# Group normalisation on one core: stores of two groups a partition from paired half buffers

## The chip, the cores and the metric

The kernel runs on one core of one Trainium2 chip. Its time is the device time of one execution in microseconds (us), and the figure given for a kernel is the median of its runs. The kernel before the change takes 633.47 us (three runs, 633.45 to 633.54). Everything else below is read from one further execution that the hardware profiler recorded; its span, from its first instruction to its last, is 632.5 us.

## What is computed

```python
def reference(x, g, b):                      # x: 128 x 1024 x 32 x 16, bf16
    G = 32
    xr = x.reshape(B, G, C // G, H, W)
    mu = xr.mean(axis=(2, 3, 4), keepdims=True)
    var = ((xr - mu) ** 2).mean(axis=(2, 3, 4), keepdims=True)
    xn = (xr - mu) / jnp.sqrt(var + 1e-5)
    xn = xn.reshape(B, C, H, W)
    return xn * g[None, :, None, None] + b[None, :, None, None]
```

Each of the 128 samples has 32 groups of 32 channels, a channel is 512 numbers, so a group is 16,384 numbers or 32 KB, and each group is normalised by its own mean and variance. 134 MB are read and 134 MB are written.

## The kernel before

One group sits on one partition. A tile is 128 groups, which is four samples, so a tile is 128 partitions by 32 KB (4 MB) and is one unbroken stretch of memory; there are 32 tiles, numbered 0 to 31. The tiles live in a pool of six buffers (XBUFS, UPFRONT), and a tile is scaled in place in its buffer.

For tile i the main loop (the last lines of the function) does this. L(i) loads the tile, in one transfer of 32 KB a partition (line 101), or in four transfers of 8 KB a partition for the first and the last tile. M(i) multiplies the tile by an identity on TensorE (PE in the profile) in 32 matmuls into one accumulator (line 166), and R0(i) sums that on VectorE (DVE, line 189): the negative mean. Q(i) squares the tile on ScalarE (ACT, line 244) in two halves. V(i) makes a scale and a shift for each channel: a square root on ACT (line 308), a reciprocal on DVE (line 312), three small operations on GpSimd (POOL, lines 337 to 353). A(i) scales 16 of the 32 channels on DVE and 13 on POOL (line 368). The last 3 are scaled on ACT in finish(i) (line 363), which then stores the tile, S(i), in one transfer of 32 KB a partition (line 381). The last two tiles are scaled and stored in quarters of 8 KB a partition within A(i).

The order of the work is written out by hand, and a helper chains the instructions of each engine in that order. In turn i of the loop come Q(i), M(i+1), R0(i+1), V(i), A(i). Two consequences matter later. finish(i) is called inside Q(i+1), between its two halves. And R0(i+1) stands before V(i) and A(i) on DVE, so the scaling of tile i waits until tile i+1 has landed and has been summed.

All large transfers are issued from one queue, that of the sync engine (SP), and each is spread over the core's 16 DMA engines, 8 partitions to each engine. Transfers start in the order of their issue. A load into a used buffer waits, on SP, until the store out of that buffer has landed on all 16 engines, and everything behind it on SP waits with it. Before the change SP's order from then on is two stores, two loads: S(24) S(25) L(30) L(31) S(26) S(27) and so on. The variable RUN is that two.

Of the kernel before, what the change touches and what calls it, by code (L numbers as in the profile page):

```python
# [9 lines left out]
ALU = mybir.AluOpType  # L10
F32 = mybir.dt.float32
BF16 = mybir.dt.bfloat16
# [2 lines left out]
NUM_GROUPS = 32  # L15
EPS = 1e-5

XBUFS = 6
UPFRONT = 6
RUN = 2  # L20
MM_FREE = 512
QUARTERS = 4
STORE_IN_PARTS = 2
# [6 lines left out]
def kernel(  # L30
# [13 lines left out]
    nc = tc.nc  # L44
    P = nc.NUM_PARTITIONS
    B0, C, H, W = x.shape
    G = NUM_GROUPS
    HW = H * W
    assert P % G == 0 and C % G == 0
    NS = P // G  # L50
    assert B0 % NS == 0
    NT = B0 // NS
    KC = C // G
    F = KC * HW
    inv_n = 1.0 / float(F)
# [2 lines left out]
    NQ = QUARTERS  # L58
    QF = F // NQ
# [1 line left out]
    MQ = NMM // NQ  # L61
    assert NQ == 4 and F % (NQ * MMN) == 0 and KC % NQ == 0

    x_v = x.rearrange("(t n) (g k) h w -> t (n g) (k h w)", n=NS, g=G)
    o_v = out.rearrange("(t n) (g k) h w -> t (n g) (k h w)", n=NS, g=G)
    g_v = g.rearrange("(g k) -> g k", g=G)
    b_v = b.rearrange("(g k) -> g k", g=G)

    consts = ctx.enter_context(tc.tile_pool(name="consts", bufs=1))
    xpool = ctx.enter_context(tc.tile_pool(name="xpool", bufs=XBUFS))  # L70
    jpool = ctx.enter_context(tc.tile_pool(name="jpool", bufs=1))
    spool = ctx.enter_context(tc.tile_pool(name="spool", bufs=4))
    pspool = ctx.enter_context(
# [2 lines left out]
    gpool = ctx.enter_context(  # L76
        tc.tile_pool(name="gpool", bufs=1, space=bass.MemoryType.PSUM)
    )
# [6 lines left out]
    def chain(key, inst):  # L85
        prev = last.get(key)
        if prev is not None:
            tc.add_manual_dep(inst.ins, prev.ins.name, nosync, reason="pipeline order")
        last[key] = inst
        return inst  # L90

    state = {}

    def L(i):
        xt = xpool.tile([P, F], BF16, name="xt")
        parts = NQ if i == 0 or i >= NT - 1 else 1
        w = F // parts
        for c in range(parts):
            chain(
                "sp",  # L100
                nc.sync.dma_start(  # L101
                    out=xt[:, c * w : (c + 1) * w], in_=x_v[i][:, c * w : (c + 1) * w]
                ),
            )
        state[i] = {"xt": xt}

    for i in range(min(UPFRONT, NT)):
        L(i)

    gb_b = consts.tile([G, 2, KC], BF16)  # L110
    chain("act", nc.scalar.dma_start(out=gb_b[:, 0, :], in_=g_v))
    chain("act", nc.scalar.dma_start(out=gb_b[:, 1, :], in_=b_v))
    eps_t = consts.tile([P, 1], F32)
# [4 lines left out]
    ones_b = consts.tile([P, P], BF16)  # L118
# [3 lines left out]
        out=eye[:],  # L122
        in_=ones_b[:],
        pattern=[[-1, P]],
# [2 lines left out]
        base=0,  # L127
        channel_multiplier=1,
    )
    rep = consts.tile([G, P], BF16)  # L130
    nc.gpsimd.affine_select(
        out=rep[:].rearrange("q (n a) -> q n a", n=NS),
        in_=ones_b[0:G, :].rearrange("q (n a) -> q n a", n=NS),
        pattern=[[0, NS], [-1, G]],
        compare_op=ALU.is_equal,
        fill=0.0,
        base=0,
        channel_multiplier=1,
    )
    gb = consts.tile([P, 2, KC], F32)  # L140
    gam = gb[:, 0, :]
    bet = gb[:, 1, :]

    def GB():
        gb_p = gpool.tile([P, 2, KC], F32, name="gb_p")
        chain(
            "pe",
            nc.tensor.matmul(  # L148
                out=gb_p[:].rearrange("p a k -> p (a k)"),
                lhsT=rep[:],  # L150
                rhs=gb_b[:].rearrange("q a k -> q (a k)"),
                start=True,
                stop=True,
            ),
        )
        chain("dve", nc.vector.tensor_copy(out=gb[:], in_=gb_p[:]))  # L156

    def shifted(i):
        return i == 0 or i == NT - 1

# [124 lines left out]
    def V(i):  # L285
        st = state[i]
        if shifted(i):
            var = spool.tile([P, 1], F32, name="var")
            jv = spool.tile([P, NQ], F32, name="jv")
            chain(  # L290
                "dve",
                nc.vector.tensor_scalar(  # L292
                    out=jv[:],
                    in0=st["sq"][:],
                    scalar1=inv_n,
                    scalar2=st["seed"][:],
                    op0=ALU.mult,
                    op1=ALU.add,
                    accum_out=var[:],
                ),  # L300
            )
            last_sum, scale, bias = var, float(NQ * NQ), eps_t
        else:
            last_sum, scale, bias = st["s1"], inv_n, st["v0"]
        rstd = spool.tile([P, 1], F32, name="rstd")
        chain(
            "act",
            nc.scalar.activation(  # L308
                out=rstd[:], in_=last_sum[:], func=ACT.Sqrt, bias=bias[:], scale=scale
            ),  # L310
        )
        chain("dve", nc.vector.reciprocal(out=rstd[:], in_=rstd[:]))  # L312
        scl = spool.tile([P, KC], F32, name="scl")
        bia = spool.tile([P, KC], F32, name="bia")
        if i == NT - 1:
            chain(
                "dve",
                nc.vector.tensor_scalar(
                    out=scl[:], in0=gam, scalar1=rstd[:], scalar2=None, op0=ALU.mult
                ),  # L320
            )
            chain(
                "dve",
                nc.vector.scalar_tensor_tensor(  # L324
                    out=bia[:],
                    in0=scl[:],
                    scalar=st["negmean"][:],
                    in1=bet,
                    op0=ALU.mult,
                    op1=ALU.add,  # L330
                ),
            )
        else:
            shift = spool.tile([P, KC], F32, name="shift")
            chain(
                "pool",
                nc.gpsimd.tensor_scalar(  # L337
                    out=scl[:], in0=gam, scalar1=rstd[:], scalar2=None, op0=ALU.mult
                ),
            )  # L340
            chain(
                "pool",
                nc.gpsimd.tensor_scalar(  # L343
                    out=shift[:],
                    in0=scl[:],
                    scalar1=st["negmean"][:],
                    scalar2=None,
                    op0=ALU.mult,
                ),
            )  # L350
            chain(
                "pool",
                nc.gpsimd.tensor_tensor(out=bia[:], in0=shift[:], in1=bet, op=ALU.add),  # L353
            )
        st["scl"], st["bia"] = scl, bia

    def scale_on(key, i, k):
        st = state[i]
        span = st["xt"][:, k * HW : (k + 1) * HW]
        scl = st["scl"][:, k : k + 1]  # L360
        bia = st["bia"][:, k : k + 1]
        if key == "act":
            inst = nc.scalar.activation(  # L363
                out=span, in_=span, func=ACT.Identity, bias=bia, scale=scl
            )
        else:
            eng = nc.vector if key == "dve" else nc.gpsimd
            inst = eng.tensor_scalar(  # L368
                out=span,
                in0=span,  # L370
                scalar1=scl,
                scalar2=bia,
                op0=ALU.mult,
                op1=ALU.add,
            )
        chain(key, inst)

    def S(i, lo, hi):
        chain(
            "sp",  # L380
            nc.sync.dma_start(
                out=o_v[i][:, lo * QF : hi * QF],
                in_=state[i]["xt"][:, lo * QF : hi * QF],
            ),
        )

    def in_parts(i):
        return i >= NT - STORE_IN_PARTS

    def A(i):  # L390

        if not in_parts(i):
            for n in range(POOL_SHARE):
                scale_on("pool", i, KC - LAST_SHARE - POOL_SHARE + n)
            for k in range(KC - LAST_SHARE - POOL_SHARE):
                scale_on("dve", i, k)
            if i + 1 < NT:
                R1(i + 1)
            return
        for c in range(NQ):  # L400
            for k in range(c * KQ, (c + 1) * KQ):
                on_act = i == NT - 1 and k >= (c + 1) * KQ - ACT_SHARE
                scale_on("act" if on_act else "dve", i, k)
            S(i, c, c + 1)
            if c == NQ // 2 - 1 and i + 1 < NT:
                R1(i + 1)

    def finish(i):
        if i < 0 or in_parts(i):
            return  # L410
        for k in range(KC - LAST_SHARE, KC):
            scale_on("act", i, k)
        S(i, 0, NQ)
        state.pop(i)
        if i % RUN == RUN - 1:
            first = i + 1 + UPFRONT - RUN
            for j in range(first, min(first + RUN, NT)):
                L(j)

    M(0)  # L420
    R0(0)
    GB()
    R1(0)
    for i in range(NT):
# [36 lines left out]
```

## Time and profile before

| | |
|---|---|
| median of the runs | 633.47 us |
| the profiled execution's span | 632.5 us |
| HBM read and written | 134.22 MB each, 424 GB/s over the span |
| busy ACT | 537.9 us (85% of the span) |
| busy DVE | 379.0 us (60%) |
| busy POOL | 345.3 us (55%) |
| busy PE | 260.9 us (41%) |
| loads of 4096 KB, issue to landing, median | 19.4 us (30 of them) |
| stores of 4096 KB, issue to landing, median | 29.3 us (30 of them) |
| loads and stores of 1024 KB | 8 each, 11.5 and 17.9 us |

Busy times are sums over the span for each engine. The time from issue to landing holds the time that a transfer spends in the queue behind earlier ones. The page also has the chain that ended last, which goes back from the last instruction to whatever released it; in this execution 62% of that chain is DMA, 15% ACT and 9% PE.

### The profile page before, as it was taken

The page shows a single profiled execution, that of the slowest core. Times are in us where ns is not written, and L with a number is a line of the kernel's source. Part 1 is how long each engine was busy: PE and PEld are TensorE (multiplying, and loading weights), DVE is VectorE, ACT ScalarE, POOL GpSimd, SP SyncE. Part 2 cuts the span into 40 slices and gives each one's busy share as a digit, 9 for nine tenths or more (in the row PEclk, how much of TensorE's full clock was granted, in tenths as well). Part 3 has the DMA queues.
Part 4 walks back from the last instruction along what each step waited for, and adds up shares of the span by engine and source line. Part 5 has one row for each costly group of instructions (what it writes and reads, how often), then busy time and mean ns, then how long its engine had stood idle before and what let it go on. Part 6 is the DMA issues. An engine that isn't in the chain of part 4 may idle for free.

```text
span 632.5 us, 3907 instructions
## 1 busy us (share of the span) xinstructions
PE 260.9 (41%) x1025; PEld 106.4 (17%) x1025; DVE 379.0 (60%) x645; ACT 537.9 (85%) x268; POOL 345.3 (55%) x523
## 2 busy tenths in 40 slices
PE   5577609064180632806327063270723607146000
PEld 2223203021030210302113021030301203012000
DVE  1077766666676477563665636666466663657660
ACT  4599999999999699696996969969798796987960
POOL 0077776666666377563665636666365663657100
PEclk9789759668595675957759577595875958758555
DMA  9999999999999999999999999999999999999996
GB/s 371 437 428 406 436 433 431 433 429 433 429 424 433 429 437 431 432 434 433 434 432 424 432 433 431 429 432 432 431 431 431 436 429 432 431 425 435 431 423 260
DMA packets 11063, 268.70 MB, mean 425 GB/s; under 512 B 1312, under 2 KB 1312, under 8 KB 1312
## 3 DMA queue, kind: packets, MB, share of 16 engines
q1 hardware_dynamic: 10944, 268.44, 99.0%
q8 instruction: 8, 0.13, 0.1%
q14 instruction: 15, 0.12, 0.0%
q10 hardware_dynamic: 96, 0.00, 0.0%
HBM read 134.22 MB, written 134.22 MB: 424 GB/s over the span
## 4 chain that ended last, share of the span: by engine, by line
DMA 62%; ACT 15%; PE 9%; issue 5%; DVE 3%; POOL 2%; SPq 0%; DVEq 0%; ACTq 0%; POOLq 0%
DMA out_dram<-xt 40%; DMA xt<-in_x_dram 21%; ACT ja L244 13%; PE pa L166 9%; DVE xt L368 3%; ACT xt L363 2%; POOL xt L368 1%; DMA gb_b<-in_g_dram 0%; ACT rstd L308 0%; POOL scl L337 0%; POOL shift L343 0%; POOL bia L353 0%; SPq L101 0%; DVE rstd L312 0%; DVE jd L189 0%
## 5 line engine op out<-in xcount | busy, mean ns | idle before, releaser
L244 ACT ACTIVATE ja<-xt,negmean 128x8192 fp8e5<-128x8192 bf16 x60 | 426.6, 7109 | 55.2 <-DVE jd L189 55.1
L166 PE MATMUL pa<-xt,eye 128*128 128x512 bf16 x976 | 250.1, 421 | 317.9 <-DMA xt<-in_x_dram 317.9
L368 DVE TENSOR_SCALAR xt<-xt,scl,bia 128x512 bf16<-128x512 bf16 x536 | 351.4, 730 | 39.8 <-POOL bia L353 39.8
L368 POOL TENSOR_SCALAR xt<-xt,scl,bia 128x512 bf16<-128x512 bf16 x390 | 307.5, 801 | 3.4 <-POOL bia L353 0.3
L166 PEld LDWEIGHTS <-eye 128*128 128x128 bf16 x1024 | 106.3, 106 | 472.2 <-DMA xt<-in_x_dram 318.8
L337 POOL TENSOR_SCALAR scl<-gb,rstd 128x32 f32<-128x32 f32 x31 | 11.1, 358 | 220.1 <-DVE rstd L312 220.1
L189 DVE TENSOR_SCALAR_CACHE_REDUCE jd<-pa 128x512 bf16<-128x512 f32 x32 | 21.9, 684 | 113.9 <-PE pa L166 113.9
L363 ACT ACTIVATE xt<-xt,bia,scl 128x512 bf16<-128x512 bf16 x98 | 72.0, 799 | 0.8 <-DVE bia L324 0.8
L312 DVE RECIPROCAL rstd<-rstd 128x1 f32<-128x1 f32 x32 | 5.2, 163 | 72.7 <-ACT rstd L308 72.7
L244 ACT ACTIVATE ja<-xt,q 128x4096 fp8e5<-128x4096 bf16 x8 | 29.7, 3706 | 6.6 <-DVE jd L189 6.4
L343 POOL TENSOR_SCALAR shift<-scl,negmean 128x32 f32<-128x32 f32 x31 | 11.1, 358 | 3.1
L216 POOL TENSOR_SCALAR off<-negmean,q 128x1 f32<-128x1 f32 x2 | 0.9, 430 | 20.4 <-DVE jd L189 20.4
L166 PE MATMUL pb<-xt,eye 128*128 128x512 bf16 x48 | 11.0, 379 | 0.6 <-DMA xt<-in_x_dram 0.6
L244 ACT ACTIVATION_READ_ACCUMULATOR ja<-xt,negmean 128x1 f32 x60 | 11.2, 187 | 0.0
L308 ACT ACTIVATE rstd<-s,v 128x1 f32<-128x1 f32 x30 | 8.8, 294 | 2.8
L353 POOL TENSOR_TENSOR bia<-shift,gb 128x32 f32<-128x32 f32 x31 | 7.8, 251 | 2.6
L273 POOL TENSOR_SCALAR v<-s 128x1 f32<-128x1 f32 x30 | 5.7, 191 | 2.5
L308 ACT ACTIVATE rstd<-var,eps_t 128x1 f32<-128x1 f32 x2 | 0.6, 294 | 7.5 <-DVE jv L292 7.5
L156 DVE COPY gb<-gb_p 128x64 f32<-128x64 f32 x1 | 0.2, 225 | 5.5 <-PE gb_p L148 5.5
L116 ACT ACT_TABLE_LOAD x1 | 1.3, 1283 | 1.7 <-PEq L445 1.7
L189 DVE DVE_READ_ACCUMULATOR jd<-pa 128x1 f32 x32 | 2.6, 80 | 0.0
L292 DVE TENSOR_SCALAR_CACHE_REDUCE jv<-sq,seed 128x4 f32<-128x4 f32 x2 | 0.4, 214 | 2.7 <-ACT ja L244 2.7
(18 smaller groups left out, 6.1 us busy)
## 6 DMA issues: line engine op xcount, KB each, us to landing
xt<-in_x_dram SPq DMA_DIRECT2D x30, 4096.0 KB, 19.4
out_dram<-xt SPq DMA_DIRECT2D x30, 4096.0 KB, 29.3
xt<-in_x_dram SPq DMA_DIRECT2D x8, 1024.0 KB, 11.5
out_dram<-xt SPq DMA_DIRECT2D x8, 1024.0 KB, 17.9
gb_b<-in_g_dram ACTq DMA_DIRECT2D x1, 2.0 KB, 3.2
gb_b<-in_b_dram ACTq DMA_DIRECT2D x1, 2.0 KB, 5.2
```

What stands on the lines that cost most here:

```text
L116: chain("act", nc.scalar.activation(out=warm[:], in_=eps_t[:], func=ACT.Sqrt))
L166: nc.tensor.matmul(out=ps[:], lhsT=eye[:], rhs=st["xt"][:, k * MMN : (k + 1) * MMN], start=(k == lo), stop=(k == hi - 1),),
L189: nc.vector.tensor_scalar(out=jd[:], in0=ps[:], scalar1=-inv_n, scalar2=seed, op0=ALU.mult, op1=ALU.add, accum_out=total[:],),
L244: nc.scalar.activation(out=ja[:, 0:w], in_=st["xt"][:, k * w : (k + 1) * w], func=ACT.Square, bias=bias, scale=scale, accum_out=sq, satura ...
L273: nc.gpsimd.tensor_scalar(out=v0[:], in0=s0[:], scalar1=inv_n, scalar2=EPS, op0=ALU.mult, op1=ALU.add,),
L308: nc.scalar.activation(out=rstd[:], in_=last_sum[:], func=ACT.Sqrt, bias=bias[:], scale=scale),
L312: chain("dve", nc.vector.reciprocal(out=rstd[:], in_=rstd[:]))
L337: nc.gpsimd.tensor_scalar(out=scl[:], in0=gam, scalar1=rstd[:], scalar2=None, op0=ALU.mult),
L343: nc.gpsimd.tensor_scalar(out=shift[:], in0=scl[:], scalar1=st["negmean"][:], scalar2=None, op0=ALU.mult,),
L353: nc.gpsimd.tensor_tensor(out=bia[:], in0=shift[:], in1=bet, op=ALU.add),
L363: inst = nc.scalar.activation(out=span, in_=span, func=ACT.Identity, bias=bia, scale=scl)
L368: inst = eng.tensor_scalar(out=span, in0=span, scalar1=scl, scalar2=bia, op0=ALU.mult, op1=ALU.add,)
```

## The change

Two groups of a sample, neighbours in memory, now share a partition. A pair of tiles covers eight samples: partition (n, q) holds the groups 2q and 2q+1 of sample n, which are 64 KB of unbroken memory. The even tile of a pair is the first 32 KB of every partition's row, the odd tile the second. A load still brings one tile, 32 KB a partition, but now from a row pitch of 64 KB in memory where it was 32 KB. The six buffers become one tile of six units side by side, so the two units of a pair are neighbours, and from tile 6 on one store of 64 KB a partition writes the two tiles of a pair together (8 MB). Tiles 0 to 5 are stored singly, and tiles 30 and 31 in quarters as before. The scale and shift constants get two sets of 32 channels, one for the even and one for the odd tile.

SP's order changes with it. Before: S(0) S(1) L(6) L(7), S(2) S(3) L(8) L(9), S(4) S(5) L(10) L(11), and so on to S(24) S(25) L(30) L(31) S(26) S(27) S(28) S(29), then the quarters. After, with P(a,b) for a pair's store: S(0) S(1) L(6) L(7) S(2) S(3) L(8) S(4) L(9) S(5) L(10) P(6,7) L(11) L(12) P(8,9) L(13) L(14), and so on to P(24,25) L(29) L(30) P(26,27) L(31) P(28,29), then the quarters. The instructions of the other engines keep their number and order.

```diff
-XBUFS = 6
-UPFRONT = 6
-RUN = 2
+UNITS = 6
+PAIR = 2
+SKEW = 2
...
-    x_v = x.rearrange("(t n) (g k) h w -> t (n g) (k h w)", n=NS, g=G)
-    o_v = out.rearrange("(t n) (g k) h w -> t (n g) (k h w)", n=NS, g=G)
+    x_v = x.rearrange("(t n) (q k) h w -> t (n q) (k h w)", n=NS, q=GQ)
+    o_v = out.rearrange("(t n) (q k) h w -> t (n q) (k h w)", n=NS, q=GQ)
...
+    ring = xpool.tile([P, UNITS * F], BF16, name="xt")
 
     def L(i):
-        xt = xpool.tile([P, F], BF16, name="xt")
-        parts = NQ if i == 0 or i >= NT - 1 else 1
+        at = i % UNITS
+        xt = ring[:, at * F : (at + 1) * F]
+        parts = NQ if i == 0 or i == NT - 1 else 1
         w = F // parts
         for c in range(parts):
+            lo = (i % PAIR) * F + c * w
             chain(
                 "sp",
                 nc.sync.dma_start(
-                    out=xt[:, c * w : (c + 1) * w], in_=x_v[i][:, c * w : (c + 1) * w]
+                    out=xt[:, c * w : (c + 1) * w],
+                    in_=x_v[i // PAIR][:, lo : lo + w],
                 ),
             )
...
         for k in range(KC - LAST_SHARE, KC):
             scale_on("act", i, k)
-        S(i, 0, NQ)
-        state.pop(i)
-        if i % RUN == RUN - 1:
-            first = i + 1 + UPFRONT - RUN
-            for j in range(first, min(first + RUN, NT)):
-                L(j)
+        if i < UNITS:
+            S(i, 0, NQ)
+            if i == 1:
+                L(UNITS)
+                L(UNITS + 1)
+            elif i > SKEW:
+                L(UNITS + i - 1)
+        elif i % PAIR == PAIR - 1:
+            t = i // PAIR
+            at = (i - 1) % UNITS
+            chain(
+                "sp",
+                nc.sync.dma_start(
+                    out=o_v[t], in_=ring[:, at * F : (at + PAIR) * F]
+                ),
+            )
+            for j in (i + UNITS - SKEW, i + UNITS - SKEW + 1):
+                if j < NT:
+                    L(j)
```

More of the change, by code (lines that the diff above doesn't have):

```diff
@@ L49 @@
     assert P % G == 0 and C % G == 0
-    NS = P // G
+    GQ = G // PAIR
+    NS = P // GQ
     assert B0 % NS == 0
-    NT = B0 // NS
+    NT = B0 * G // P
+    NB = NT // PAIR
     KC = C // G
@@ L62 @@
     assert NQ == 4 and F % (NQ * MMN) == 0 and KC % NQ == 0
-    x_v = x.rearrange("(t n) (g k) h w -> t (n g) (k h w)", n=NS, g=G)
-    o_v = out.rearrange("(t n) (g k) h w -> t (n g) (k h w)", n=NS, g=G)
-    g_v = g.rearrange("(g k) -> g k", g=G)
-    b_v = b.rearrange("(g k) -> g k", g=G)
+    x_v = x.rearrange("(t n) (q k) h w -> t (n q) (k h w)", n=NS, q=GQ)
+    o_v = out.rearrange("(t n) (q k) h w -> t (n q) (k h w)", n=NS, q=GQ)
+    g_v = g.rearrange("(q k) -> q k", q=GQ)
+    b_v = b.rearrange("(q k) -> q k", q=GQ)
     consts = ctx.enter_context(tc.tile_pool(name="consts", bufs=1))
-    xpool = ctx.enter_context(tc.tile_pool(name="xpool", bufs=XBUFS))
+    xpool = ctx.enter_context(tc.tile_pool(name="xpool", bufs=1))
     jpool = ctx.enter_context(tc.tile_pool(name="jpool", bufs=1))
@@ L105, in L @@
         state[i] = {"xt": xt}
-    for i in range(min(UPFRONT, NT)):
+    for i in range(min(UNITS, NT)):
         L(i)
-    gb_b = consts.tile([G, 2, KC], BF16)
+    gb_b = consts.tile([GQ, 2, PAIR * KC], BF16)
     chain("act", nc.scalar.dma_start(out=gb_b[:, 0, :], in_=g_v))
@@ L129 @@
     )
-    rep = consts.tile([G, P], BF16)
+    rep = consts.tile([GQ, P], BF16)
     nc.gpsimd.affine_select(
         out=rep[:].rearrange("q (n a) -> q n a", n=NS),
-        in_=ones_b[0:G, :].rearrange("q (n a) -> q n a", n=NS),
-        pattern=[[0, NS], [-1, G]],
+        in_=ones_b[0:GQ, :].rearrange("q (n a) -> q n a", n=NS),
+        pattern=[[0, NS], [-1, GQ]],
         compare_op=ALU.is_equal,
@@ L139, with gam, bet @@
     )
-    gb = consts.tile([P, 2, KC], F32)
-    gam = gb[:, 0, :]
-    bet = gb[:, 1, :]
+    gb = consts.tile([P, 2, PAIR * KC], F32)
+    def gam(i):
+        h = i % PAIR
+        return gb[:, 0, h * KC : (h + 1) * KC]
+    def bet(i):
+        h = i % PAIR
+        return gb[:, 1, h * KC : (h + 1) * KC]
     def GB():
-        gb_p = gpool.tile([P, 2, KC], F32, name="gb_p")
+        gb_p = gpool.tile([P, 2, PAIR * KC], F32, name="gb_p")
         chain(
@@ L318, in V @@
                 nc.vector.tensor_scalar(
-                    out=scl[:], in0=gam, scalar1=rstd[:], scalar2=None, op0=ALU.mult
+                    out=scl[:], in0=gam(i), scalar1=rstd[:], scalar2=None, op0=ALU.mult
                 ),
@@ L327, in V @@
                     scalar=st["negmean"][:],
-                    in1=bet,
+                    in1=bet(i),
                     op0=ALU.mult,
@@ L337, in V @@
                 nc.gpsimd.tensor_scalar(
-                    out=scl[:], in0=gam, scalar1=rstd[:], scalar2=None, op0=ALU.mult
+                    out=scl[:], in0=gam(i), scalar1=rstd[:], scalar2=None, op0=ALU.mult
                 ),
@@ L352, in V @@
                 "pool",
-                nc.gpsimd.tensor_tensor(out=bia[:], in0=shift[:], in1=bet, op=ALU.add),
+                nc.gpsimd.tensor_tensor(out=bia[:], in0=shift[:], in1=bet(i), op=ALU.add),
             )
@@ L381, in S @@
             nc.sync.dma_start(
-                out=o_v[i][:, lo * QF : hi * QF],
+                out=o_v[i // PAIR][
+                    :, (i % PAIR) * F + lo * QF : (i % PAIR) * F + hi * QF
+                ],
                 in_=state[i]["xt"][:, lo * QF : hi * QF],
```

## The prediction, made before the changed kernel ran

> **What bounds the kernel now.** I read the page's busy shares and its DMA slices first, then the sync queue's timeline, then the windows of the last microseconds.
>
> ```profile
> DMA  9999999999999999999999999999999999999996
> GB/s 371 437 428 406 436 433 431 433 429 433 429 424 433 429 437 431 432 434 433 434 432 424 432 433 431 429 432 432 431 431 431 436 429 432 431 425 435 431 423 260
> ...
> q1 hardware_dynamic: 10944, 268.44, 99.0%
> q8 instruction: 8, 0.13, 0.1%
> ```
>
> The DMA engines are busy in every slice but the last, at a flat 431 GB/s. ACT, the busiest compute engine, has 85%. So the transfers are the bound. Each load and each store of a tile is a "slot" of the queue, 64 in all, and the time is 64 slots plus the ends.
>
> ```profile
> 230.23 10.01 SPq L101 DMA_DIRECT2D xt<-in_x_dram  x2
> 240.34 0.85 SPq L381 DMA_DIRECT2D out_dram<-xt  x2
> 269.62 9.95 SPq L101 DMA_DIRECT2D xt<-in_x_dram  x2
> ...
> 543.36 11.42 SPq L101 DMA_DIRECT2D xt<-in_x_dram  x5
> 554.94 60.10 SPq L381 DMA_DIRECT2D out_dram<-xt  x12
> ```
>
> A load is issued when the store out of its buffer has landed, so these starts clock the queue: 151.97 to 543.36 us is ten turns of four slots, 9.78 us a slot on the slowest engine. The two stores behind the loads go out at once (0.85 us for both): they were ready, and about 19 us of loads still lie queued ahead of them. No compute shows on this path.
>
> ```profile
> 622.00:624.00 2.00, 0.00 (x0) 0.00 (x0) 0.00 (x0) 0.00 (x0) 0.00 (x0) 0.50 1.00 422
> 624.00:626.00 2.00, 0.00 (x0) 0.00 (x0) 0.00 (x0) 0.00 (x0) 0.00 (x0) 0.50 0.69 291
> 626.00:628.00 2.00, 0.00 (x0) 0.00 (x0) 0.00 (x0) 0.00 (x0) 0.00 (x0) 0.50 0.32 135
> 628.00:630.00 2.00, 0.00 (x0) 0.00 (x0) 0.00 (x0) 0.00 (x0) 0.00 (x0) 0.50 0.17 70
> 630.00:632.50 2.50, 0.00 (x0) 0.00 (x0) 0.00 (x0) 0.00 (x0) 0.00 (x0) 0.50 0.04 16
> ```
>
> (The last two columns are the DMA share and GB/s.) The 16 engines do not end together: the share falls from 624 on. The trace's landing records, one for each engine and transfer, have the last transfer landing from 624.18 (first engine) to 631.54 us (last). The lag grows through the run, about 1 us per 78 us, the beat of queue q8's eight 16 KB instruction fetches. So the slowest engine sets the end, and it is never idle; the others have up to 7 us in hand.
>
> **The change, part by part.**
>
> *Longer store packets.* The packet records of the trace give a 32 KB packet a median of 1213 ns, an 8 KB one 309 ns, a semaphore write 9 ns. Four short packets are 23 ns more than one long one, 7.7 ns for each packet taken away. The landings say less: a store of 32 KB rows takes 9.66 us (S(26) to S(29)), one in four quarters 9.78 us, so 24 packets and 3 semaphore writes an engine cost 0.12 us. A pair store drops 8 packets and one semaphore write, a third of that, 0.04 us; by the packets it is 8 x 7.7 + 9 = 70 ns; at the least, if the row were cut in two again, 9 ns. Twelve pair stores: 0.1 to 0.85 us. I take 0.035 x 12 = 0.4 us, by the landings, since they are what the queue advances by. More can't come from here: 4.19 MB at 9.66 us is already 434 GB/s.
>
> The Trainium skill (DMA: Bandwidth & Descriptors, "Anatomy of one DMA") gives each GpSimd-issued DMA a fixed 2.0 us beside its bytes. Twelve transfers fewer would then be 24 us, but the landings here lie 9.66 us apart back to back, so that cost is hidden.
>
> *Loads at twice the row pitch.* No 32 KB load at that pitch is in the trace. Packets of loads and stores have the same median, at pitch 32 KB, and I take no cost. Nearest row above: L(31) in quarters, a quarter of each row at a time, took 9.87 us against 9.71 for a whole load, 0.16 us more, extra packets included; over 31 loads 5.0 us. Below: the load's gap to a store, 9.71 - 9.66 = 0.05, times 31, a gain of 1.6 us, if the pitch removed it.
>
> The same page ("Latency and other measured facts") speaks against this change: large power-of-two row pitches slow HBM copies, 207 GB/s for 214 at 512 KiB, the mildest it lists. An estimate by that loss is 31 x 9.71 x 0.033 = 9.9 us; 64 KB isn't listed, and no run here shows it.
>
> *The new queue order.* What counts is whether each pair store is issued before the loads ahead of it run out. A pair store waits for its odd tile, and behind it on SP wait the next two loads, and behind those all later compute. How long an odd tile takes from landing to issue:
>
> ```profile
> 562.79 11.48 PE L166 MATMUL pa<-xt,eye 128*128 128x512 bf16 x40 [22.01 <-DMA xt<-in_x_dram]
> 572.58 0.69 DVE L189 TENSOR_SCALAR_CACHE_REDUCE jd<-pa 128x512 bf16<-128x512 f32 x1 [9.72 <-PE pa L166]
> 573.32 7.12 ACT L244 ACTIVATE ja<-xt,negmean 128x8192 fp8e5<-128x8192 bf16 x1 [6.33 <-DVE jd L189]
> 582.55 7.11 ACT L244 ACTIVATE ja<-xt,negmean 128x8192 fp8e5<-128x8192 bf16 x1
> 591.62 5.26 DVE L368 TENSOR_SCALAR xt<-xt,scl,bia 128x512 bf16<-128x512 bf16 x16 [1.28 <-POOL bia L353]
> ```
>
> This is tile 30, landed at 562.75. A first load after a gap takes 8.4 to 9.8 us on PE (the other first ones of the trace); I take 9.2. Then 0.76 to ACT's start, 18.30 from there to the scaling's start (573.32 to 591.62, two halves of squares, three columns of the tile before, scale and shift), 11.11 for 16 columns on DVE while POOL shares the work (574.64 to 585.75), 0.14 to the issue, and 0.04 at the front: 39.55 us. From issue to first packet with an empty queue: 1.02 us at the kernel's start on SP (0.79 to 1.81), 1.43 on ACT. I take 1.02: 40.6 us.
>
> In the steady run the slowest engine has, after an odd load, the even load, a pair store, two more loads: 9.7 + 19.3 + 9.7 + 9.7 = 48.4 us. Covered by 7.8. The first pair, P(6,7): ACT ends tile 7 near 149.3, plus 12.9 for its scaling is 162.2, and L(10) ends at 171.3 by before's landings. Covered by 8.
>
> The last pair isn't. Between P(26,27) and P(28,29) stands only L(31), since there is no L(32). From L(29)'s landing: L(30) 9.7 + P(26,27) 19.3 + L(31) 9.9 = 38.9 us, against 40.6. The slowest engine idles 1.7 us (0.9 to 2.7 by the PE and issue bounds). L(29) lands after 56 slots, 553.0 us before, 552.6 with the saving, so P(28,29) goes out near 592.2, where S(28) and S(29) went out at 562.9 and 585.9. Late next: tiles 30 and 31 by 6.3 us (ACT starts tile 30 behind tile 29). The last quarter, 614.7 before, is issued at 621.0 and due near 629; without that cover it would add directly. A fetch of 0.7 us in the tail stays.
>
> *Constants and everything else.* Two sets of 32 channels, a 128-wide copy where it was 64: once, behind 62 us of loads, nothing. Same instructions elsewhere.
>
> **Sum.** 632.5 + 1.7 - 0.4 = 633.8 us of span. The runs lie 0.97 above it: 634.8 us, 0.2% up.
>
> **Rivals.**
> B. The last wait is hidden: tile 29 gets through PE in 8.4 and the packet starts at once. Only packets count: 633.5 - 0.4 = 633.1. For: the idle is 1.7 in 40.6. Against: it needs two low values together.
> C. Faster: an instruction fetch holds its engine up less among longer packets. Place: the slowest engine's 7.4 us of lag; it decides once more than 2.6 of it are gone (634.8 to 632.2). Half gone, 3.7, gives 631.1. Against: the fetched bytes remain.
> D. Strided loads cost: half of the bound, 634.8 + 2.5 = 637.3; all of it, 639.8. Against: packet time looks set by the engine, equal both ways.
> E. The change doesn't do it: 64 KB rows travel as two packets. 634.8 + 0.3 = 635.1.
>
> **How the numbers follow.** Forecast 0.50, B 0.22, C 0.07, D 0.13, E 0.08. A change under 0.2% (1.27 us) can hardly be told from none: below 632.2 faster, above 634.74 slower. The forecast lies on that edge, its own range 633.9 to 635.9: 0.28 slower, 0.22 same. D and most of E are slower, B same: slower 0.48, same 0.44, faster 0.08. Range 632.6 to 638.3, most of D included.
>
> **What would show it.** Packets of q1: 9216 if rows go whole, 10752 if cut. A dip of the DMA share near 585 to 593 instead of after 624, since the engines in front now wait there and all end together; P(28,29) issued near 592. If loads land over 9.71 us apart it is D; if the lag at L(29) is well under 6 us, C. Wrong altogether if a pair store is late in the middle of the run.

## The result and the profile after

The changed kernel takes 635.9 us (median of six runs, 635.17 to 636.81) against 633.5 us before in the same comparison: a ratio of 1.0037, with a 95% interval of 1.0025 to 1.0048. It is slower by 2.4 us. The profiled execution is the slowest of the six: its time is 636.81 and its span 635.1 us, 2.6 us over the span before. The page, transfers first:

```profile
DMA  9999999999999999999999999999999999998698
GB/s 364 429 428 429 430 433 433 438 427 429 436 421 431 458 411 448 418 435 448 413 447 415 444 442 415 458 411 448 415 427 451 421 454 413 442 434 356 284 420 365
...
q1 hardware_dynamic: 9216, 268.44, 98.4%
q8 instruction: 8, 0.13, 0.1%
```

There are 9216 packets where there were 10944, so the 64 KB rows travel whole. The bytes are the same. For 36 slices of about 15.9 us the rate is as flat on average as before (a packet is counted whole in the slice in which it starts, hence the zigzag). Then come two weak slices, 356 and 284 GB/s, and a last slice that is stronger than before (365 for 260). The sync queue's timeline near the end shows what was issued around the weak slices (start, duration, engine, line, what):

```profile
542.77 0.33 SPq L106 DMA_DIRECT2D xt<-in_x_dram  x1
552.72 0.34 SPq L439 DMA_DIRECT2D out_dram<-xt  x1
553.11 3.97 SPq L106 DMA_DIRECT2D xt<-in_x_dram  x4
592.76 0.34 SPq L439 DMA_DIRECT2D out_dram<-xt  x1
600.89 20.72 SPq L393 DMA_DIRECT2D out_dram<-xt  x8
```

The five rows are L(30), P(26,27), the four parts of L(31), P(28,29), and the eight quarter stores. After L(31) the queue gets nothing for 36 us. The windows around 585 us (the last columns are the granted clock, the DMA share and GB/s) show the engines run dry:

```profile
575.00:580.00 5.00, 0.00 (x0) 0.00 (x0) 1.25 (x4) 4.91 (x4) 0.13 (x1) 0.50 0.88 372
580.00:585.00 5.00, 0.59 (x2) 0.28 (x3) 3.68 (x7) 5.00 (x1) 4.42 (x8) 0.50 0.97 403
585.00:590.00 5.00, 5.00 (x16) 1.85 (x14) 5.00 (x7) 5.00 (x6) 5.00 (x7) 0.60 0.31 126
590.00:594.00 4.00, 3.73 (x18) 1.38 (x15) 3.23 (x7) 4.00 (x1) 2.03 (x4) 1.00 0.64 270
```

(The windows count a packet at its start too, so the last row says little: the packets of P(28,29) start at 593.6.) From 585 to 590 the engines are busy for less than a third of their time on average: the first is through with L(31) at 584.80, the last at 591.78. Why the store was late is read in the timeline of tile 29:

```profile
552.49 16.82 PE L178 MATMUL pa<-xt,eye 128*128 128x512 bf16 x64 [22.31 <-DMA xt<-in_x_dram]
562.44 0.69 DVE L201 TENSOR_SCALAR_CACHE_REDUCE jd<-pa 128x512 bf16<-128x512 f32 x1 [9.84 <-PE pa L178]
563.17 7.12 ACT L256 ACTIVATE ja<-xt,negmean 128x8192 fp8e5<-128x8192 bf16 x1 [6.48 <-DVE jd L201]
572.41 7.11 ACT L256 ACTIVATE ja<-xt,negmean 128x8192 fp8e5<-128x8192 bf16 x1
581.48 11.14 DVE L380 TENSOR_SCALAR xt<-xt,scl,bia 128x512 bf16<-128x512 bf16 x16 [1.29 <-POOL bia L365]
```

(The first row holds the 32 matmuls of tile 30 as well; those of tile 29 end at 562.41.) PE waited 22.31 us for the load, which landed at 552.45. Each row starts as the one above lets it go, and the scaling ends at 592.62, 0.14 us before the issue. The only work in this chain that isn't tile 29's is that of ACT on three columns of tile 28 (2.21 us from 570.29), between the two halves of the squares.

The landing records of the two profiles (first and last of the 16 engines, us) put the loss in its place:

```
                              before              changed
L(29) landed                  -     to 553.00*    545.86 to 552.45
L(31), last quarter, landed   565.96 to 572.62    584.80 to 591.78
S(27) landed                  585.30 to 591.99    -
P(28,29) landed               -                   613.40 to 613.57
last store landed             624.18 to 631.54    633.32 to 634.09
* the same number of slots done (S(25) there)
```

### The profile page after: what moved, and what is told of

It is laid out like the page before. It is cut to its first block, busy times and chain, and to the rows that moved or that the text cites. A ratio compares the mean times of both kernels' runs of the same rounds, so it can differ in the third digit from the quotient of the medians.

```text
span 635.1 us, 3870 instructions
## 1 busy us (share of the span) xinstructions
PE 269.3 (42%) x1025; PEld 108.6 (17%) x1025; DVE 379.9 (60%) x645; ACT 537.9 (85%) x268; POOL 346.4 (55%) x523
## 3 DMA queue, kind: packets, MB, share of 16 engines
q1 hardware_dynamic: 9216, 268.44, 98.4%
## 4 chain that ended last, share of the span: by engine, by line
DMA 42%; ACT 26%; DVE 12%; PE 9%; issue 7%; POOL 1%; SPq 1%; DVEq 0%; ACTq 0%; POOLq 0%
DMA xt<-in_x_dram 34%; ACT ja L256 22%; DVE xt L380 11%; PE pa L178 9%; DMA out_dram<-xt 7%; ACT xt L375 4%; ACT rstd L320 0%; POOL scl L349 0%; POOL shift L355 0%; SPq L106 0%; SPq L439 0%; POOL bia L365 0%; DVE rstd L324 0%; DVE jd L201 0%; DVE jv L304 0%
## 5 line engine op out<-in xcount | busy, mean ns | idle before, releaser
L178 PE MATMUL pa<-xt,eye 128*128 128x512 bf16 x976 | 257.0, 430 | 324.4 <-DMA xt<-in_x_dram 320.9
L178 PEld LDWEIGHTS <-eye 128*128 128x128 bf16 x1024 | 108.6, 108 | 484.2 <-DMA xt<-in_x_dram 324.6
L178 PE MATMUL pb<-xt,eye 128*128 128x512 bf16 x48 | 12.6, 426 | 0.0
```

The lines of the kernel that those rows point to most:

```text
L178: nc.tensor.matmul(out=ps[:], lhsT=eye[:], rhs=st["xt"][:, k * MMN : (k + 1) * MMN], start=(k == lo), stop=(k == hi - 1),),
```

## The experiments

The theory W is the prediction's: the last pair store is late. Its rivals are P (loads or quarter stores cost more at the doubled row pitch) and K (64 KB packets cost more than two of 32 KB). Ratios are to the kernel before in the same comparison; its medians there were 633.71, 633.93 and 633.77 us.

**The last pair apart.** In the changed kernel:

```diff
-        if i < UNITS:
+        if i < UNITS or i >= NT - 2 * PAIR:
             S(i, 0, NQ)
-            if i == 1:
+            if i >= UNITS:
+                pass
+            elif i == 1:
```

> The changed kernel, but tiles 28 and 29 are stored singly, tile 28 as soon as it is ready; the other eleven pair stores stay. Theory W (the last pair store is late, about 2.3 us of empty queues): tile 28 goes out near 576 us and covers the wait for tile 29, so 633.1 us (633.5 less 0.4). Rival P (loads, or quarter stores, cost more at a row pitch of 64 KB) and rival K (64 KB packets cost more): 635.5 to 635.9 us, since nearly all of either remains.

Measured: 633.41 us (ratio 0.9995, interval 0.9986 to 1.0003). The loss is gone. Its sync queue's timeline and its windows:

```profile
574.96 17.36 SPq L393 DMA_DIRECT2D out_dram<-xt  x2
...
580.00:585.00 5.00, 1.13 (x3) 0.43 (x4) 4.28 (x7) 5.00 (x1) 4.81 (x8) 0.50 1.04 431
585.00:590.00 5.00, 5.00 (x18) 1.94 (x17) 5.00 (x7) 5.00 (x6) 5.00 (x7) 0.70 1.09 464
590.00:594.00 4.00, 3.14 (x14) 1.09 (x12) 2.44 (x6) 4.00 (x1) 1.23 (x3) 1.00 0.96 414
```

Tile 28 went out at 574.96, 17.8 us ahead of the pair, and the DMA engines stay busy through 594. Eleven pair stores and all strided loads are still there, so P and K can hold little of the loss.

**The pitch alone.** The changed layout, with the loop of before:

```diff
-        if i < UNITS:
-            S(i, 0, NQ)
...
+        S(i, 0, NQ)
+        if i % PAIR == PAIR - 1:
+            first = i + 1 + UNITS - PAIR
+            for j in range(first, min(first + PAIR, NT)):
+                L(j)
```

> The kernel before with the changed layout alone: rows of 32 KB at a pitch of 64 KB for loads and stores, single stores, the queue order of before. W: as before, 633.5 us within 0.5. P: 635 to 636 us, the whole loss. K: as before.

Measured: 633.92 us (ratio 1.0001, interval 0.9992 to 1.0010). P falls: rows of 32 KB at a pitch of 64 KB cost nothing that shows, in loads or stores.

**The order with 32 KB packets, first try.** In the changed kernel:

```diff
-            chain(
-                "sp",
-                nc.sync.dma_start(
-                    out=o_v[t], in_=ring[:, at * F : (at + PAIR) * F]
-                ),
-            )
+            S(i - 1, 0, NQ)
+            S(i, 0, NQ)
```

> The changed kernel with every pair store cut into two stores of 32 KB rows, issued one after the other when the pair is ready; layout and queue order stay the changed ones. W: the wait stays and the packets' gain of 0.4 us is lost: 636.0 to 636.4 us. P: as the changed kernel, 635.9. K: the loss goes, 633.5 to 634 us.

Measured: 634.09 us (ratio 1.0006, interval 0.9997 to 1.0015). W's number is missed by 2 us, and the result looks like K's. The edit was at fault: two stores wait separately, so tile 28's store needn't wait for tile 29. The timeline shows it:

```profile
575.17 17.32 SPq L393 DMA_DIRECT2D out_dram<-xt  x2
```

Tile 28 left at 575.17 as in the first experiment; this kernel lacks the wait that it should have kept. It says only that the order without the wait costs nothing clear of scatter.

**The order with 32 KB packets, second try.** The edit is shown against the first try:

```diff
+            S(i, 0, NQ)
             S(i - 1, 0, NQ)
-            S(i, 0, NQ)
```

> As the kernel with every pair store cut into two stores of 32 KB rows, but the odd tile's store is issued ahead of the even tile's, so that the even one can no longer go out early. W: the last pair waits as in the changed kernel and the packets' gain (0.4 to 0.7 us) is lost: 636.2 to 636.7 us. K: 633.5 to 634.1 us, as there are no 64 KB packets.

Measured: 636.03 us (ratio 1.0034, interval 1.0022 to 1.0047), 2 us above the first try, with the same bytes in the same packets and only the even tile held back. Its sync queue, from the four parts of L(31) on:

```profile
553.61 3.58 SPq L106 DMA_DIRECT2D xt<-in_x_dram  x4
591.19 28.89 SPq L393 DMA_DIRECT2D out_dram<-xt  x10
```

Nothing is issued between 557.2 and 591.19. K falls. The time is just under W's number, and 0.13 us from that of the changed kernel (below), well inside the scatter of either, so the packets' gain doesn't show here.

**The changed kernel again**, beside the last one.

> The changed kernel unaltered, beside the others on one chip. W: 635.9 us, within 0.7, as measured.

Measured: 635.9 us (ratio 1.0034, interval 1.0022 to 1.0046).

**The wait made shorter and longer.** In the changed kernel, for tile 29 alone, 8 channels on DVE and 6 on POOL fewer or more:

```diff
-            for n in range(POOL_SHARE):
-                scale_on("pool", i, KC - LAST_SHARE - POOL_SHARE + n)
-            for k in range(KC - LAST_SHARE - POOL_SHARE):
-                scale_on("dve", i, k)
+            for n in range(POOL_SHARE - 6 * (i == NT - 3)):
+                scale_on("pool", i, KC - LAST_SHARE - POOL_SHARE + n % POOL_SHARE)
+            for k in range(KC - LAST_SHARE - POOL_SHARE - 8 * (i == NT - 3)):
+                scale_on("dve", i, k % (KC - LAST_SHARE - POOL_SHARE))
```

> The changed kernel, but 14 of the 32 channels of tile 29 are left unscaled (8 on VectorE, 6 on GpSimd), which makes the last pair store ready some 5 us earlier with the same transfers. W: the wait is covered, 633.1 to 633.6 us. P and K: 635.9 us, no transfer changes.

Measured: 633.35 us (ratio 0.9995, interval 0.9986 to 1.0004). With + in place of - before the 6 and the 8:

> The changed kernel, but 14 channels of tile 29 are scaled a second time (8 more instructions on VectorE, 6 on GpSimd; the output of those channels is not the reference's), which delays the last pair store by about 5.5 us. W: the whole delay shows, 635.9 + 5.5 = 641.4 us. Rival, that the tail isn't on the path: 635.9 us.

Measured: 640.85 us (ratio 1.0108, interval 1.0093 to 1.0123). The pair's issue in the light and in the heavy kernel:

```profile
587.62 0.34 SPq L439 DMA_DIRECT2D out_dram<-xt  x1
```

```profile
597.08 0.34 SPq L439 DMA_DIRECT2D out_dram<-xt  x1
```

The heavy one's issue is 4.32 us later than the changed kernel's 592.76, and its span is 639.4 - 635.1 = 4.3 us longer: one for one. In the light one the packets start at 588.47, before the last engine is through with L(31) at 591.0, and the loss is gone. The foremost engine had landed L(31) at 584.81 and did run dry, but it isn't the one that sets the end. The kernel before with the heavy edit:

> The kernel before with the same 14 channels of tile 29 scaled a second time. W: the store of tile 29 was issued 18 us ahead of its turn there, so the time stays at 633.5 us. Rival, that the compute tail sets the end in both kernels: about 639 us.

Measured: 633.85 us (ratio 0.9999, interval 0.9990 to 1.0009). Its store of tile 29 is the first of the three in the second row; the first row is that of the kernel before:

```profile
585.89 0.33 SPq L381 DMA_DIRECT2D out_dram<-xt  x1
...
589.74 7.44 SPq L381 DMA_DIRECT2D out_dram<-xt  x3
```

The store goes out 3.85 us later and the time doesn't change: the queue has S(28) left, whose landing on the last engine comes at 601.72.

**The engines' lag.** Theory F in the text below is the prediction's remark on the beat of queue q8's fetches, which rival C builds on. In the kernel before:

```diff
-            matmuls(st, "pa", 0, NMM)
+            matmuls(st, "pa", 0, NMM // 2)
```

> The kernel before with 16 of the 32 matmuls of tiles 1 to 30 left out (the mean is of half a tile, so the output is not the reference's). Theory F of the prediction: the slowest DMA engine lags by about 7 us because TensorE's instruction fetches, eight of 16 KB, all pass through it; half as many instructions is four fetches, so the last engine's lag falls to about 3.5 us and the time to about 630 us. Rival: the lag is the engine's own, not the fetches'; then 633.5 us.

Measured: 634.54 us (ratio 1.0008, interval 0.9999 to 1.0018). Its page:

```profile
q14 instruction: 15, 0.12, 0.0%
q8 instruction: 4, 0.07, 0.0%
```

The fetches of q8 were halved, yet the last transfer still lands from 624.53 to 631.91, a lag of 7.38 us where the kernel before has 7.36. Theory F falls. The 15 instruction packets of 8 KB on queue q14 are as many as before; whether they hold engines up was not tried, and what does stays open.

**The last pair apart, again.**

> The changed kernel with tiles 28 and 29 stored singly, a second time, to see whether it is faster than the kernel before by the packets' gain: 0.3 to 0.7 us below it. Rival: no different from it, the gain being taken back by the single slots that are left.

Measured: 633.39 us (ratio 0.9994, interval 0.9985 to 1.0003). Both times the median is 0.3 to 0.4 us below the kernel before, and both intervals reach just past 1. A gain of that size fits the packets' term, but these times don't prove it. The landings speak for it: the 56th slot of the queue (L(29), or S(25) in the order of before) has landed on the last engine at 551.89 to 552.45 us in the six profiles with 64 KB stores, and at 552.44 to 553.37 in the six without.

## Why the prediction was right, and where its sizes were off

It forecast 634.8 us, slower by 1.3, through one place: P(28,29) issued late because no L(32) stands ahead of it. The place and the mechanism are shown, by the issue at 592.76 (592.2 was forecast), by the dip before 593.6, and by the experiments that removed, shortened and lengthened the wait. The size was 2.4 instead of 1.3 (2.1 in the repeat). That the range holds the result says little: it reached from 632.6 to 638.3 to take in the strided loads of rival D, and the prediction gave "slower" only 0.48 against 0.44 for "same". Point by point, with "the last engine" for the one that lands last:

- *Longer packets.* A 64 KB packet has a median of 2418 ns against 2 x 1213, a gain of 8 ns, as the 8 KB and 32 KB packets had said. L(29) landed at 552.45, 0.55 us earlier than the same slot before; 0.4 was taken for all twelve. Between profiles of one kernel that landing moves by as much (551.89 in the repeat), so the size is rough.
- *Loads at twice the pitch.* Taken as nothing. Right: the pitch alone made no difference that shows, and 32 KB packets keep their 1213 ns. The loss that the Trainium skill (DMA: Bandwidth & Descriptors, "Latency and other measured facts") lists for pitches of 512 KiB and more doesn't show at 64 KB.
- *Cover in the middle.* P(6,7) was forecast ready at 162.2 and went out at 164.52, with L(10) landing at 172.13; P(26,27) went out 9.4 us before L(30) had landed. By the landing records no store before the last pair is late.
- *The last pair's wait.* From L(31)'s landing on the last engine to the first packet the queue stood for 593.60 - 591.78 = 1.82 us, close to the 1.7 forecast, but by luck: both sides of that difference were half a microsecond too small. Tile 29 took 40.31 us from landing to issue, 0.76 more than the 39.55 forecast, nearly all of it in the matmuls (9.92 us from the first start to the last end, for the 9.2 taken; the bound was 9.8); from issue to first packet it was 0.84 us, not 1.02; in all 41.15 for 40.6. And the cover, L(30), P(26,27) and L(31), took 591.78 - 552.45 = 39.33 us for 38.9, because P(26,27) took 19.72 us on the last engine. Before, the same stretch of the queue took 553.00 to 591.99, or 38.99 us: 0.34 more now.
- *What a landing leaves out.* The sum counts the idle time from a landing, and an engine's last packet ends earlier: that of L(31) at 591.33, so the last engine moved nothing for 593.60 - 591.33 = 2.27 us. Back to back this costs nothing: before, the last packet of S(27) ended at 591.53 and its landing was recorded at 591.99, by which time S(28) was under way. These 0.46 us the sum put at zero.
- *After the restart.* That the rest of the tail would run as before was the other term put at zero. From the last packet of S(27) to the last landing it took 631.54 - 591.53 = 40.01 us before; from the first packet of P(28,29) it took 634.09 - 593.60 = 40.49 us: 0.48 more. What the records show of it stands in the last section.
- *The sum*, in the profiled run: - 0.55 + 0.34 + 1.82 + 0.46 + 0.48 = 2.55 us, against 634.09 - 631.54 = 2.55 between the last landings. This is one pair of profiles, and the changed one is the slowest of its six runs. In the repeat, 635.77 us, tile 29 took 39.80 us, the queue stood for 1.33 us after the landing, and the last landing came at 633.03.
- *Late next.* The last quarter was forecast at 621.0 and went out at 621.28, inside its cover, as forecast.
- *The rivals.* B (the wait hidden) and E (rows cut in two) fell with the trace, D (strided loads) with the pitch-only kernel. C did not happen: at L(29) the lag was 552.45 - 545.86 = 6.6 us. Its premise, that the fetches cause the lag, is refuted as far as q8's go; it wasn't part of the forecast's sum.

## What to carry to other kernels

Where the transfers are the bound, as here, ask first whether each is issued before the ones ahead of it are through. Merging two stores ties the first to the second's readiness; here that was for a gain of about half a microsecond at best, and it cost more than that at the one place where the queue ahead was a slot shorter. Look for that place at the ends of the loop, where a load is missing. When you work out such a gap, count it from the last packet to the first and not from a landing. And ask of an edit that splits a transfer what each half now waits for: two stores are not one store cut in two.

## What was not expected of the hardware

After the 16 DMA engines have run dry and started together (first packets at 593.60 to 593.74), their packets are slower. In the tail of the changed kernel a 64 KB store packet has a median of 2434 ns, 2418 earlier in the run; an 8 KB one 313 ns, where the kernel before, whose engines were spread over 7 us, has 309. In the 32 KB kernel with the late order a 32 KB one has 1220 against 1213. From first packet to end the tail took 40.49 us, 40.50 in the repeat, 40.45 in the heavy kernel (597.92 to 638.37) and 40.59 in the late one (592.03 to 632.62), against 40.01 before. By the medians, 8 x 16 + 64 x 4 ns = 0.38 us of the difference would be the packets.

Two more rows bear on it. One engine falls behind in this tail: it lands the second quarter 3.68 us after the first (616.04 to 619.72), while an 8 KB instruction packet of queue q14 starts at 618.36, and it is the one that ends last. From there its quarters land 2.43 us apart, as before the change, and those of the foremost engine 2.49. Before, the last engine had a stop of this kind too, in S(29), which took it 10.52 us for the 9.66 of the first. So slower packets and a different stop are both in the 0.48 us, and their shares are open. That starting together makes the packets slower was not tried by itself; with loads it doesn't show, for at the kernel's start the engines land within 0.5 us of each other, and a 32 KB load packet there has a median of 1213 to 1215 ns.
